# A tuned attention-and-gate kernel: the first x tile in halves, rstd by a GpSimd power, and h chunks begun on two token tiles

**Chip, cores, metric.** One core of one Trainium2 chip. The time is the device time of one execution in microseconds (us), as the median of several executions; "span" is the part of it that the profiler covers, from the first to the last instruction. In the kernel before, the time is the span plus some 1.7 us in every execution.

## The reference

x is 2048 tokens by 448 columns in bf16. The result is x + s·g, where both branches read the same LayerNorm of x:

```python
xn = layernorm(x)                       # eps 1e-5
q, k, v = split_heads(xn @ wqkv)        # 16 heads of 28
phi = lambda t: where(t > 0, t + 1, exp(t)) + 1e-6
kv, z = sum_s phi(k) v, sum_s phi(k)    # linear attention, not causal
s = (phi(q) @ kv / (phi(q)·z + 1e-6)) @ wo
h = relu(xn @ w1 + b1) ** 2             # 448 -> 1792
g = silu(h @ w2 + b2)                   # 1792 -> 448
out = x + s * g
```

## The kernel before

A small list scheduler written in Python takes operations with their reads, writes and estimated durations and fixes the order on each engine, and which of the eight PSUM banks each accumulation gets. The main block is groups of four accumulations, shared among K and Q projections (`K0` = keys of token tile 0) and h chunks (`H4` = columns 512 to 639 of h for 512 tokens). The contraction over 448 columns is three steps of 128 rows and one of 64; two accumulations run their 64-row steps in pairs, on the two halves of the array.

The part that the change touches is the head: what must happen before that block can begin. (Cuts are marked `...`; the comments behind `#` are mine.)

```python
add("dve", lambda e, _: e.memset(junk[:, :], 0.0), [], ["junk"], 0.2).prio = -1000
...
def ln_rstd(lo, hi):                       # rstd = exp(-0.5 * ln(var + eps)), both on ScalarE
    add("act", ... activation(out=vep[:, c], in_=mv[:, c, 1], func=AF.Ln, bias=eps5[:, 0:1]) ...)
    add("act", ... activation(out=rstd[:, c], in_=vep[:, c], func=AF.Exp, scale=-0.5) ...)
...
def pe_transpose(si, eng, prio):           # one token tile of xn -> xT, by TensorE
    for c in range(3):
        e.transpose(v[:, c * P : (c + 1) * P], xn[:, si, c * P : (c + 1) * P], ident[:, :])
    e.transpose(v[0:64, 3 * P : 4 * P], xn[:, si, 384:448], ident[:, :])       # the last 64 columns twice,
    return e.transpose(v[64:P, 3 * P : 4 * P], xn[:, si, 384:448], ident[:, :])  # once for each array half
    ...                                    # then the copy PSUM -> xT, on ScalarE or VectorE (eng)
...
order = ["st0", "mv0", "st1", "mv1", "xn0", "st2", "xn1", "mv2", "st3", "mv3", "xT1", "xn2", "xn3", "xT2", "xT3"]
...
warm(10, wide=True)                        # ten 512-column matmuls on junk, for the clock
pe_transpose(0, "act", -100)
warm(2)                                    # two 128-column ones
pe_transpose(1, "dve", at_head["xT1"])

def third_and_fourth():
    pe_transpose(2, "act", -100)
    pe_transpose(3, "dve", at_head["xT3"])

pe_two(kk(0), kk(1), third_and_fourth)     # K0, K1; tiles 2 and 3 stand before their last steps
...
streams = (("H0 H1 H2 H3 K2 H4 K3 H6", ...   # the first groups of four of the block
```

Three names recur below. T0 to T3 are the transposes of the token tiles. K0 and K1 are the first real matmuls. "K2" is the first matmul of the second group, which comes after chunks 0 to 3; from there on both kernels run the same work in the same order. "The hole" is the gap ahead of chunks 4 and 6, which need PSUM banks that chunks 0 to 3 give back.

## Time and profile before

| quantity | value | from |
|---|---|---|
| time, median of the rounds with the changed kernel | 147.98 us (147.73 to 148.15, 4 runs) | timing |
| span of the profiled run | 146.15 us | page |
| first statistics / K0 / K1 / K2 start | 3.72 / 6.92 / 7.59 / 12.69 us | timeline |
| hole before chunks 4 and 6 | 0.12 us | timeline, worked out below |
| K2 to the last TensorE instruction (its modelled end less the prediction's 0.163 us of pipeline) | 129.94 us | trace |

The chain and the strips stand in the prediction. What it doesn't show is how the h block passes to the second group. The timeline: start, duration, engine, line, operation, how many, and in brackets the idle time before it and what ended it.

```profile
12.24 2.42 ACT L660 ACTIVATE r<-pb,b1f 128x512 bf16<-128x512 f32 x4 [0.81 <-PE pb L651]
...
12.69 0.92 PE L601 MATMUL pb<-w_qkv,xT 64*128 64x448 bf16 x8
...
13.56 1.04 PE L651 MATMUL pb<-xT,w 64*128 64x512 bf16 x8
```

Matmul durations overlap, so spacing must be read from starts: four pairs of 448 columns at 0.189 us follow K2 and take 0.756 us, thus chunk 4 could start at 13.45 and does at 13.56. That 0.12 is the hole: ScalarE, which began to empty the first chunks' banks at 12.24, needs some 0.6 us for each.

### The profile page before, as it was taken

What the parts mean: (1) busy time and instruction counts of PE and PEld (TensorE: products, weight loads), DVE (VectorE), ACT (ScalarE), POOL (GpSimd) and SP (SyncE); (2) the same over time, 40 slices, a digit from 0 to 9 for tenths busy, and PEclk for the clock granted to TensorE, in tenths of its full rate; (3) what the DMA queues carried; (4) which work ended last, traced back from release to release, by engine and by line L of the source; (5) the groups of instructions that cost most, each with busy time, mean ns of one, the idle gap of its engine ahead of it and who ended that gap; (6) DMA issues with size and microseconds to landing.
All of it is one profiled execution on the core that took longest, in us unless ns stands there. A gap on an engine that the chain in (4) does not pass through costs nothing.

```text
span 146.1 us, 3240 instructions
## 1 busy us (share of the span) xinstructions
PE 141.3 (97%) x1330; PEld 69.2 (47%) x1330; DVE 97.2 (67%) x224; ACT 79.8 (55%) x154; POOL 21.2 (14%) x39
## 2 busy tenths in 40 slices
PE   6999999999999999999999999999999999999990
PEld 2344446644444446443545535545555555555440
DVE  0979688888978995999995594973052341604583
ACT  3557799889887888889797191613030220301310
POOL 6000000000000000008900000000050505144140
PEclk9999999999999999999999999999999999999999
DMA  4997649995301100000000000000001011020122
GB/s 124 307 332 215 161 88 350 307 204 112 72 4 36 36 4 0 0 0 4 0 0 0 4 0 0 7 0 0 0 17 51 31 36 63 0 65 2 63 94 94
DMA packets 15513, 10.54 MB, mean 72 GB/s; under 512 B 7244, under 2 KB 15116, under 8 KB 15500
## 3 DMA queue, kind: packets, MB, share of 16 engines
q1 hardware_dynamic: 15040, 9.89, 26.5%
q10 hardware_dynamic: 460, 0.46, 0.9%
q8 instruction: 10, 0.16, 0.5%
q14 instruction: 3, 0.02, 0.1%
HBM read 6.94 MB, written 1.84 MB: 60 GB/s over the span
## 4 chain that ended last, share of the span: by engine, by line
PE 93%; DVE 3%; DMA 2%; issue 0%; DVEq 0%
PE pb L651 29%; PE pb L852 29%; PE pb L601 7%; PE pb L912 7%; PE pb L683 6%; PE pb L623 6%; DMA x_tok<-in_A_x_dram 2%; PE pb L638 1%; DVE st L447 1%; PE pb L689 1%; PE pb L830 1%; PE pb L775 1%; PE pb L741 1%; PE pb L803 1%; PE pb L930 1%; PE pb L490 1%
## 5 line engine op out<-in xcount | busy, mean ns | idle before, releaser
L651 PE MATMUL pb<-xT,w 64*128 64x512 bf16 x392 | 51.6, 376 | 0.1
L852 PE MATMUL pb<-w,r 64*128 64x448 bf16 x448 | 48.2, 349 | 0.0
L660 ACT ACTIVATE r<-pb,b1f 128x512 bf16<-128x512 f32 x56 | 35.0, 689 | 9.0 <-PE pb L651 8.9
L852 PEld LDWEIGHTS pb<-w,r 64*128 64x128 bf16 x448 | 22.8, 94 | 21.0 <-PE pb L852 0.6
L651 PEld LDWEIGHTS pb<-xT,w 64*128 64x128 bf16 x392 | 21.7, 94 | 21.7 <-ACT r L660 0.7
L870 ACT ACTIVATE gbuf<-gbuf 128x448 bf16<-128x448 bf16 x15 | 8.3, 577 | 35.7 <-DVE gbuf L860 35.7
L860 DVE TENSOR_TENSOR gbuf<-pb,b2b 128x448 bf16<-128x448 f32 x15 | 8.7, 621 | 25.4 <-PE pb L852 25.4
L899 POOL TENSOR_TENSOR obuf<-obuf,x_tok 128x448 bf16<-128x448 bf16 x12 | 12.1, 1029 | 57.4 <-DVE obuf L889 57.4
L601 PE MATMUL pb<-w_qkv,xT 64*128 64x448 bf16 (+1 forms) x106 | 16.0, 350 | 0.0
L623 PE MATMUL pb<-xT,w_qkv 64*128 64x512 bf16 x84 | 15.6, 376 | 0.0
L668 DVE TENSOR_TENSOR r<-r 128x512 bf16<-128x512 bf16 x37 | 13.7, 443 | 0.0
L912 PE MATMUL pb<-msb,pqT 64*128 64x448 bf16 x90 | 13.6, 349 | 0.0
L669 ACT ACTIVATE r<-r 128x512 bf16<-128x512 bf16 x19 | 11.3, 633 | 0.0
L447 DVE BATCH_NORM_STATS2 st<-x_tok 128x6 f32<-128x448 bf16 x16 | 9.4, 611 | 2.5 <-DMA x_tok<-in_A_x_dram 2.5
L889 DVE TENSOR_TENSOR obuf<-pb,gbuf 128x448 bf16<-128x448 f32 (+1 forms) x17 | 9.6, 593 | 2.2 <-PE pb L852 1.7
L579 ACT ACTIVATE pk<-pb 128x448 bf16<-128x448 f32 x16 | 8.1, 540 | 3.6 <-PE pb L601 2.9
L591 DVE SCALAR_TENSOR_TENSOR pk<-pb,pk 128x448 bf16<-128x448 f32 x16 | 9.8, 622 | 0.4
L378 POOL MEMSET ehd<- 128x896 bf16 x1 | 0.8, 844 | 62.9 <-DVE zb L613 62.9
L839 DVE TENSOR_TENSOR pqT<-pqT,pb 128x512 bf16<-128x512 bf16 x12 | 7.7, 684 | 3.1 <-PE pb L830 3.1
L683 PE MATMUL pb<-pk,xn 128*128 128x448 bf16 x48 | 9.6, 353 | 0.0
L601 PEld LDWEIGHTS pb<-w_qkv,xT 64*128 64x128 bf16 (+1 forms) x106 | 6.8, 94 | 5.1 <-DVE xT L500 0.4
L623 PEld LDWEIGHTS pb<-xT,w_qkv 64*128 64x128 bf16 x84 | 6.3, 94 | 4.3
(90 smaller groups left out, 117.5 us busy)
## 6 DMA issues: line engine op xcount, KB each, us to landing
out_dram<-obuf SPq DMA_DIRECT2D x15, 112.0 KB, 1.7
w<-in_B_w_dram SPq DMA_DIRECT2D x1, 1568.0 KB, 9.5
x_tok<-in_A_x_dram SPq DMA_DIRECT2D x3, 448.0 KB, 4.4
w_qkv<-in_A_wqkv_dram SPq DMA_DIRECT2D x3, 336.0 KB, 4.8
w<-in_B_w_dram SPq DMA_DIRECT2D x2, 384.0 KB, 4.6
w<-in_B_w_dram SPq DMA_DIRECT2D x1, 576.0 KB, 5.7
w_o<-in_A_wo_dram SPq DMA_DIRECT2D x1, 392.0 KB, 10.8
w_qkv<-in_A_wqkv_dram SPq DMA_DIRECT2D x6, 56.0 KB, 4.3
```

The costliest lines, as they stand in the source:

```text
L447: "dve", lambda e, _: e.bn_stats(st6[:, si, :], x_tok[:, si, :]), [("x", si)], [("st", si)], 0.553
L591: lambda e, _: e.scalar_tensor_tensor(out=slot, in0=ps(buf)[0:rows, 0:n], scalar=1.0 + 1e-6, in1=slot, op0=ALU.add, op1=ALU.max),
L601: return e.matmul(ps(b)[:, 0:D], xT[half[h], c, si * P : (si + 1) * P], w_qkv[half[h], c, D : 2 * D], start=start, stop=stop,)
L623: return e.matmul(ps(b)[:, 0:512], w_qkv[half[h], c, m * P : (m + 1) * P], xT[half[h], c, g * 512 : (g + 1) * 512], start=start, stop=stop,)
L651: return e.matmul(ps(b)[:, 0:512], w_1[half[h], c, fi * P : (fi + 1) * P], xT[half[h], c, g * 512 : (g + 1) * 512], start=start, stop=stop,)
L660: lambda e, _: e.activation(out=slot, in_=ps(b)[:, 0:512], func=AF.Relu, bias=b1f[:, fi : fi + 1]),
L668: return e.tensor_tensor(out=slot, in0=slot, in1=slot, op=ALU.mult)
L669: return e.activation(out=slot, in_=slot, func=AF.Square)
L683: last = e.matmul(ps(b)[:, 0:D], xn[:, si, c * P : (c + 1) * P], pk[:, si, :], start=(si == 0), stop=(si == NT - 1),)
L852: return e.matmul(ps(b)[:, 0:D], r2[half[h], fi, si * P : (si + 1) * P], w_2[half[h], fi, :], start=start, stop=stop)
L899: eng, lambda e, _: e.tensor_tensor(out=ob, in0=ob, in1=x_tok[:, si, :], op=ALU.add),
L912: return e.matmul(ps(b)[:, 0:D], q, msb[half[h], k, :], start=start, stop=stop)
```

## The change

The intent is to shorten the head. Its parts: (1) the warm-up matmuls read a constant that exists from the start, so VectorE needn't fill `junk`, and there are 9 wide and 4 narrow ones in place of 10 and 2; (2) the first x tile is loaded as two halves of 64 partitions on two queues; (3) rstd comes from two GpSimd operations, an add and a power, for every tile; (4) all four transposes of a tile are on 128 columns, GpSimd copying the twin of the last 64, and every copy to xT is on ScalarE; (5) four h chunks begin on the 256 tokens of tiles 0 and 1, between the transposes of tiles 2 and 3, and take the other 256 tokens afterwards. The order of VectorE's head is forced. The diff's core:

```diff
-        load_x(0, 1, "act")
+        for eng, r in (("sp", half[0]), ("act", half[1])):
+            dma(eng, x_tok[r, 0, :], x_r[r, 0, :], [("x", 0, r.start)], 64 * D * 2)
...
-                "act", ... activation(out=vep[:, c], in_=mv[:, c, 1], func=AF.Ln, bias=eps5[:, 0:1]), ...
-                "act", ... activation(out=rstd[:, c], in_=vep[:, c], func=AF.Exp, scale=-0.5), ...
+                "pool", ... tensor_scalar_add(vep[:, c], mv[:, c, 1], 1e-5), ...
+                "pool", ... tensor_tensor(out=rstd[:, c], in0=vep[:, c], in1=power[:, 0 : hi - lo], op=ALU.pow), ...
...
+            part((0, 1, 2), [("xn", si)])
+            part((3,), [("xd", si), b])          # xd: the twin columns, copied by GpSimd
...
-        warm(10, wide=True)
-        pe_transpose(0, "act", -100)
-        warm(2)
-        pe_transpose(1, "dve", at_head["xT1"])
...
-        pe_two(kk(0), kk(1), third_and_fourth)
+        warm(9, wide=True)
+        pe_transpose(0, -100)
+        warm(4)
+        pe_transpose(1, -100)
+        first = [hh(0, fi, 0) for fi in range(4)]                   # tokens 0 to 255
+        second = [hh(0, fi, 1, first[fi].bank) for fi in range(4)]  # tokens 256 to 511, same banks
+        mains(k0)
+        mains(k1)
...
+        mains(first[0])
+        pe_transpose(2, -100)
+        mains(first[1])
+        mains(first[2])
+        pe_transpose(3, -100)
+        mains(first[3])
+        rests(k0, k1, True, True)
...
+        pe_four(*second)
...
-            ("H0 H1 H2 H3 K2 H4 K3 H6", "H5 ...
+            ("K2 H4 K3 H6", "H5 ...
```

## The prediction

> **What bounds the kernel now.** I read the page's busy shares first, then the strip of forty slices, then the chain of waits over the first 14 us, then the timeline of the head. From the page:
>
> ```profile
> PE 141.3 (97%) x1330; PEld 69.2 (47%) x1330; DVE 97.2 (67%) x224; ACT 79.8 (55%) x154; POOL 21.2 (14%) x39
> ...
> PE   6999999999999999999999999999999999999990
> ...
> DVE  0979688888978995999995594973052341604583
> ACT  3557799889887888889797191613030220301310
> ...
> PE 93%; DVE 3%; DMA 2%; issue 0%; DVEq 0%
> ```
>
> The reader should see that TensorE never rests after the first slice, and that 93% of the chain that ended last is TensorE. Start-to-start spacing proves this better than busy time: from 9.65 us on, a 512-column pair of half-array matmuls follows the next every 0.216 us and a 448-column pair every 0.189 us. I laid every matmul end less a fixed 0.163 us of pipeline against the next start; from 9.65 us to the last one at 142.6 us the holes add up to 2.4 us, and most of those are 0.09 us changes of array layout. So the kernel is a head, a solid TensorE block of 133 us, and a tail of some 3.5 us. Only the head has slack to win. A head shortened by x moves the whole block by x, if the block's own inputs come earlier too.
>
> The chain in the head, in order of time:
>
> ```profile
> 0.81 2.89 DMA x_tok<-in_A_x_dram
> ...
> 3.72 0.64 DVE st L447
> ...
> 4.38 0.18 DVE mv L450
> 4.57 0.52 DVE st L447
> ...
> 5.11 0.18 DVE mv L450
> 5.29 0.28 DVE xn L469
> 5.58 0.54 DVE st L447
> 6.11 0.31 DVE xn L469
> ...
> 6.98 1.35 PE pb L601 x6
> 8.33 0.17 PE pb L490 x3
> ...
> 9.17 0.43 DVE xT L500
> ...
> 9.65 3.20 PE pb L651 x28
> ```
>
> The first x tile takes 2.89 us to land; statistics and normalisation of two tiles follow; K0 and K1 (the six L601 matmuls) start at 6.9 us; then TensorE transposes tiles 2 and 3 and, at 9.17, waits for their copy, because the first h chunks (L651) need all four tiles. The rstd link, and the first copy, stand in the timeline:
>
> ```profile
> 4.60 0.29 ACT L458 ACTIVATE vep<-mv,eps 128x1 f32<-128x1 f32 x1 [0.83 <-DVE mv L450]
> ...
> 4.93 0.20 ACT L462 ACTIVATE rstd<-vep 128x1 f32<-128x1 f32 x1
> ...
> 5.90 0.24 PE L491 MATMUL pb<-ident,xn 128*64 128x128 bf16 x1
> ...
> 6.19 0.60 ACT L501 ACTIVATE xT<-pb 128x512 bf16<-128x512 bf16 x1 [0.33 <-PE pb L492]
> ...
> 7.15 0.39 DVE L500 COPY xT<-pb 128x512 bf16<-128x512 bf16 x1
> ```
>
> **What the Trainium skill says.** (1) "TensorE: Matmul & The Clock Gate", Part 1: a cold array passes N columns in N/1.2 ns, a warm one in N/2.4 plus 2.5 ns, and it warms after a window of about 3.4 us that is not tied to the kernel's start. The trace agrees: the warm-up matmuls are 0.427 us apart, later 512-column ones 0.216, and the full clock is recorded from 5.56 us. (2) "SBUF — State Buffer", "Can I just issue two DMAs to hit both halves?": two concurrent DMAs on the two partition halves came out only 6% faster than one. So halves should win little; no run here shows it yet. (3) "Perfetto Trace Analysis", GPSIMD Engine Instruction: reported GpSimd spans are unreliable, start-to-start spacing is the measure. Here four dependent 128x32 selects on GpSimd fill 1.05 us, thus 0.26 each. (4) "SBUF — State Buffer", "Who interferes with whom": a VectorE op in a two-port mode excludes GpSimd from the port pair for its whole length. The normalisation is such a candidate; the statistics are not. The old trace has no GpSimd work beside it, so it cannot say.
>
> **The change part by part.**
>
> Warm-up: the junk memset on VectorE (0.27 us, TensorE released at 1.25) goes, since the ones constant exists before the program starts. TensorE can begin near 0.9; nine matmuls of 0.427 end at 4.8 instead of 5.7. That takes nothing off the path: transposes waited for data at 5.63.
>
> First x tile: 57 KB on each of two queues instead of 112 KB on one. Old landings: 3.70 for tile 0 on ACT's queue, 3.53 for tile 1 on SP's. Since the fixed part dominates, I take 3.4 for the later half, 0.3 earlier; statistics start at 3.4.
>
> rstd: two ScalarE ops take from the end of mv, 4.56, to the start of xn, 5.21: 0.65 us. Two dependent GpSimd ops of 0.26 (the selects' spacing; one element should cost less, a power more) plus hops make about 0.6. I call it even, slightly better. The new VectorE order is st0 mv0 st1 xn0, with mv1 behind xn0, saving 0.10. By the old spacings (st to mv 0.66, mv to st 0.11): mv0 ends 4.24, xn0 starts 4.85 and ends 5.2 (old 5.57).
>
> Transposes on 128 columns: the two 64-column ones cost a layout change of 0.09 us before and 0.12 after. The twin columns they now need come from a GpSimd copy of 128x64; a 128x128 copy there took 0.46, so I estimate 0.3 plus a hop, 0.35. So T0's last transpose runs at 5.6, its eviction 5.85 to 6.45, and K0 begins at 6.55 (old 6.92). K's weights landed at 6.1 before, so they are just not in the way.
>
> Second tile: mv1 follows xn0 (0.29 later) and ends at 5.3; 0.6 on, xn1 at 5.9 (old 6.03). st2 sits before it and needs tiles 2 and 3, old landing 5.29. The twin 0.35, the transposes, and an eviction now on ScalarE at 0.60 instead of VectorE's 0.39, put xT1 at 7.57 (old 7.54), so K1 starts at 7.68 (old 7.59). Here nearly all of the gain made so far is lost again.
>
> Order of TensorE: this is the part that wins. From K1's start the old head needs 7.59 to 12.69 = 5.10 us to reach K2. In the new order the first 256 columns of four h chunks are placed among the transposes of tiles 2 and 3, so that those tiles' LayerNorm and eviction is hidden. Warm work from K1 on: K1 3x0.189 = 0.57; bias transpose 0.06; four chunks of 3x0.109 = 1.31; T2 and T3 8x0.056 = 0.44; one layout change 0.10; K rests 0.19; h rests 2x0.109 = 0.22; second columns 14x0.109 = 1.53. Sum 4.42. Total h work is unchanged: 1.31 + 0.22 + 1.53 = 3.06 against 14x0.216 = 3.02. I add 0.2 for w1 (its last piece landed at 8.03, just where H0 wants it, and SP has one issue more ahead of it) and for xT3. K2 then begins at 7.68 + 4.62 = 12.3 instead of 12.69: 0.4 us won.
>
> Beyond the head: ScalarE drops twenty tiny ops, 4.9 us of its 79.8, and gets two xT evictions, 1.2, and two more squares, 1.3. VectorE loses two copies, the memset and two squares (about 1.9 us). Both are near 85% busy from 9.65 to 66 us under a full TensorE, so this only makes the block safer. One hole of 0.12 us at 13.56, a PSUM bank waiting for an h eviction, may go or move. Tail unchanged. Sum: about -0.4 for the head and -0.1 for such holes.
>
> **The rivals.**
> - K1 replaced by a worse wait: if the power costs 0.6 us or more, or the two-port normalisations shut GpSimd out, each of rstd0 and rstd1 slips by 0.3 to 0.5, the twins too, and K1 starts at 8.3 or later; the head then ends where it did or later: 147.9 to 148.5. For it: no GpSimd power stands in the old trace. Against: only one or two elements per partition, and VectorE is in statistics meanwhile.
> - w1 becomes the bound: in the old trace the DMA engines are saturated from 4.5 us on (near 320 GB/s), so w1's first block cannot come much before 8.0. Should it slip by 0.4 behind the additional issue, H0 starts at 8.4 and I lose 0.2: 147.6. This also caps what a faster rstd could bring, for everything after K1 stands behind H0.
> - The array stays cold longer: the warm-up is 0.4 us shorter, starts earlier and leaves a pause of 0.5 us before the first transpose. If the clock's window ends later than K0's start, the six K matmuls cost up to 1.1 us more: 148.3. The small spread of the old runs (147.73 to 148.08) speaks against a strongly phase-dependent start.
> - Everything goes well: the halves land at 3.2, GpSimd's pair takes 0.4 in place of 0.6. K1 starts at 7.2 and K2 at 11.9: 147.0.
>
> **Range and chances.** 147.88 - 0.5 gives 147.4. The rivals span 147.0 to 148.5, with the favourable side likelier as an easy 0.3 us stands in the second tile; 8 in 10 for 146.8 to 148.0. Two per cent is 2.96 us; TensorE from K2 on to the end, 133 us, is untouched, so to win it the head would have to lose a third of its 9 us, while a loss of 3 us needs a disorder down the block. Hence 0.02, 0.97, 0.01.
>
> **What would show it.** Right if x's first statistics start near 3.4 us; the mv-to-xn link is near 0.6; K0 starts near 6.5 and K1 near 7.7; TensorE shows no hole over 0.3 us from H0 to K2, and K2's first matmul stands 0.3 to 0.6 us earlier than 12.69 while the spacing after it is the same. Wrong if K2 moves by one amount and the span by another (then the block has taken or given time), if the full clock comes after 7 us, or if H0 waits on w1 by more than 0.3 us.

## The result, and the profile after

The changed kernel took 149.81 us in the median (149.18 to 151.11, 4 runs) against 147.98 (147.73 to 148.15, 4 runs) for the kernel before. The ratio is 1.0137 with a 95% interval of 1.009 to 1.0185: slower, by less than 2%, and outside the predicted 146.8 to 148.0.

The profiled spans are 147.89 and 146.15, 1.74 us apart. First the strips of the changed kernel's page, in forty slices of 3.7 us:

```profile
PE   7499999999999999999999999999999999999990
...
POOL 2566202100310000005920000000040505044140
PEclk9959999999999999999999999999999999999998
```

and the clock strip of the kernel before:

```profile
PEclk9999999999999999999999999999999999999999
```

TensorE's second slice is 4 tenths busy where it was 9, GpSimd is busy there where it wasn't, and in the third slice the granted clock, at 9 in all forty slices before, shows 5. Then the chain of waits of the changed kernel (start, length, what):

```profile
0.82 2.44 DMA x_tok<-in_A_x_dram
...
3.36 0.64 DVE st L454
...
4.02 0.20 DVE mv L455
4.21 0.08 issue
4.29 0.24 POOL vep L462
4.54 0.07 issue
4.61 0.59 POOL rstd L467
5.20 0.03 issue
5.23 0.41 DVE xn L474
...
5.69 0.24 POOL xn L485
5.93 0.20 POOL vep L462
...
6.20 0.59 POOL rstd L467
...
6.82 0.41 DVE xn L474
...
7.88 2.31 PE pb L608 x6
...
13.98 1.27 ACT r L671 x2
15.25 0.05 issue
15.30 0.82 PE pb L662 x5
```

Three things stand out. GpSimd's pair (L462, L467) is on the chain twice, once for each of the first two tiles. The six K matmuls take 2.31 us where the same six took 1.35. And the chain now passes through two ScalarE evictions (`ACT r`) into chunk 4. The timeline says what TensorE did meanwhile:

```profile
5.68 0.53 PE L500 MATMUL pb<-ident,xn 128*128 128x128 bf16 x4 [1.36 <-DVE xn L474]
...
7.27 0.61 PE L500 MATMUL pb<-ident,xn 128*128 128x128 bf16 x4 [0.83 <-DVE xn L474]
...
7.79 2.40 PE L608 MATMUL pb<-w_qkv,xT 128*128 128x448 bf16 x6
...
14.10 0.92 PE L608 MATMUL pb<-w_qkv,xT 64*128 64x448 bf16 x8
...
15.30 1.04 PE L662 MATMUL pb<-xT,w 64*128 64x512 bf16 x8 [0.28 <-ACT r L671]
```

It waited 1.36 us for the first tile and 0.83 for the second. K2 starts at 14.10, 1.41 later than before. The hole is 15.30 − (14.10 + 0.756) = 0.44, before 0.12. From K2 to the end TensorE needs 130.27 us, before 129.94. So the whole difference of 1.74 is 1.41 at K2 and 0.33 in the hole, and nothing else in the 130 us after it.

The clock is read in stretches. In the trace, it rose to full at 3.65, fell to half at 7.06 and rose again at 10.47: steps of 3.41 us. The busy times by stretch, for those two (length, then the busy time of PE, PEld, DVE, ACT and POOL with their counts, the granted clock, DMA share and GB/s):

```profile
3.65:7.06 3.41, 1.43 (x11) 0.55 (x9) 2.26 (x7) 1.23 (x2) 1.83 (x5) 1.00 1.08 317
7.06:10.47 3.41, 3.20 (x13) 1.59 (x14) 1.75 (x7) 0.74 (x2) 2.03 (x7) 0.50 0.98 312
```

A step in which TensorE was busy for 1.43 of 3.41 us was followed by one at half clock. In the kernel before, the step from 5.56 has 3.31 of 3.41.

### The profile page after: what moved, and what is told of

Its sections match the earlier page's. It is cut to its first block, busy times and chain, and to the rows that moved or that the text cites. A ratio compares the mean times of both kernels' runs of the same rounds, so it can differ in the third digit from the quotient of the medians.

```text
span 147.9 us, 3266 instructions
## 1 busy us (share of the span) xinstructions
PE 141.1 (95%) x1343; PEld 70.6 (48%) x1343; DVE 94.8 (64%) x219; ACT 77.9 (53%) x138; POOL 31.3 (21%) x64
## 4 chain that ended last, share of the span: by engine, by line
PE 92%; DMA 2%; DVE 2%; POOL 1%; ACT 1%; issue 0%; DVEq 0%
PE pb L662 29%; PE pb L865 29%; PE pb L608 7%; PE pb L925 7%; PE pb L696 6%; PE pb L630 6%; DMA x_tok<-in_A_x_dram 2%; PE pb L645 1%; PE pb L702 1%; PE pb L843 1%; ACT r L671 1%; PE pb L788 1%; POOL rstd L467 1%; PE pb L500 1%; PE pb L754 1%; PE pb L816 1%
## 5 line engine op out<-in xcount | busy, mean ns | idle before, releaser
L662 PE MATMUL pb<-xT,w 64*128 64x512 bf16 (+2 forms) x408 | 52.3, 365 | 0.3 <-ACT r L671 0.3
L662 PEld LDWEIGHTS pb<-xT,w 64*128 64x128 bf16 (+1 forms) x408 | 23.1, 94 | 21.1 <-ACT r L671 1.0
L608 PE MATMUL pb<-w_qkv,xT 64*128 64x448 bf16 (+1 forms) x106 | 17.0, 362 | 0.0
L679 DVE TENSOR_TENSOR r<-r 128x512 bf16<-128x512 bf16 x35 | 13.1, 444 | 1.3 <-ACT r L671 1.3
L680 ACT ACTIVATE r<-r 128x512 bf16<-128x512 bf16 x21 | 12.6, 636 | 0.0
L474 DVE TENSOR_SCALAR xn<-x_tok,mv,rstd 128x448 bf16<-128x448 bf16 x16 | 5.8, 394 | 5.7 <-POOL rstd L467 5.6
```

The source lines that it names most:

```text
L608: return e.matmul(ps(b)[:, 0:D], xT[half[h], c, si * P : (si + 1) * P], w_qkv[half[h], c, D : 2 * D], start=start, stop=stop,)
L662: return e.matmul(ps(b)[:, c0 : c0 + n], w_1[half[h], c, fi * P : (fi + 1) * P], xT[half[h], c, t : t + n], start=start, stop=stop,)
L679: return e.tensor_tensor(out=slot, in0=slot, in1=slot, op=ALU.mult)
L680: return e.activation(out=slot, in_=slot, func=AF.Square)
```

## The experiments

The theory after reading the two traces: two costs, each making the other larger. GpSimd's power makes the mv-to-xn link long (1.03 us, from 4.20 to 5.23, where it was 0.65), twice in series; and the shorter, earlier warm-up leaves TensorE idle in front of it, so that the clock falls back. The rivals: that one of the two does all of it, that the halved load delays the loads behind it, and that the new order of TensorE is itself bad. "The kernel before" in each set is its median in the same rounds.

### First set: the pauses, and ScalarE's rstd

**a_warm**: the changed kernel with TensorE's pauses filled.

```diff
-        warm(9, wide=True)
+        warm(12, wide=True)
         pe_transpose(0, -100)
-        warm(4)
+        warm(14)
```

> The changed kernel with the pauses of TensorE before K0 filled: 12 wide warm-up matmuls instead of 9, and 14 narrow ones instead of 4 between the first two transposes; nothing else. Theory 'clock' (TensorE fell back to the half clock at 7.06 us because it idled in the window before, so that K0, K1 and the bias transpose took 2.5 us instead of 1.2): the clock stays full from its first rise, and the time falls by 1.0 to 1.3 us, from 149.8 to about 148.6; the spread between runs shrinks. Rival 'chain' (the slow GpSimd rstd alone sets the start of K0 and the clock is only a symptom that costs nothing): no change, 149.6 to 150.0, or worse by the overshoot of the fillers.

Measured: 148.93 (148.78 to 149.16, 6 runs) against 147.86, ratio 1.0068 (1.0054 to 1.0083). The same stretch as above is now:

```profile
3.65:7.06 3.41, 3.41 (x23) 1.83 (x22) 2.27 (x7) 1.18 (x2) 1.82 (x5) 1.00 1.01 310
```

In this run the clock rose only at 6.26, so that stretch is not one of its own clock steps; the step after its rise is

```profile
6.26:9.67 3.41, 3.29 (x33) 2.08 (x32) 1.59 (x6) 1.38 (x3) 2.17 (x7) 1.00 0.93 285
```

The clock stayed full from 6.26 on, and K2 moved from 14.10 to 13.30. Over the kernel before, 1.83 became 1.07, so the pauses cost 0.76; the spread of the runs went from 1.9 to 0.4. More than half of the loss remains, so the clock isn't the whole of it.

**a_act**: the changed kernel with rstd on ScalarE again, for all tiles, warm-up as changed.

```diff
-                "pool", ... tensor_scalar_add(vep[:, c], mv[:, c, 1], 1e-5) ...
-                "pool", ... tensor_tensor(out=rstd[:, c], in0=vep[:, c], in1=power[:, 0 : hi - lo], op=ALU.pow) ...
+                "act", ... activation(out=vep[:, c], in_=mv[:, c, 1], func=AF.Ln, bias=eps5[:, 0:1]) ...
+                "act", ... activation(out=rstd[:, c], in_=vep[:, c], func=AF.Exp, scale=-0.5) ...
```

> The changed kernel with rstd back on ScalarE (logarithm and exponential) for all tiles; the warm-up stays at 9 and 4. Theory 'chain': the link from the end of mv to the start of xn falls from 1.03 us to 0.65, twice on the path, K0 starts 0.8 us earlier (7.0), and the time falls by 0.8 to about 149.0. Theory 'clock' adds: with shorter pauses the clock may hold, in some or all runs, then 147.4 to 147.9; if it falls back, 149. So a spread over 1 us between runs would itself speak for the clock.

Measured: 150.37 (149.81 to 151.41, 6 runs), ratio 1.0173 (1.0146 to 1.02): a miss, it got worse. The clock fell back here too, over 8.16 to 11.57, after this stretch:

```profile
4.75:8.16 3.41, 1.93 (x16) 0.94 (x15) 2.56 (x9) 2.20 (x7) 0.47 (x2) 1.00 0.95 276
```

So ScalarE's rstd alone doesn't save the clock. Here the second tile's link was not free to shorten: in VectorE's forced order the statistics of tiles 2 and 3 stand ahead of xn1 and waited for their load:

```profile
6.10 0.63 DVE L454 BATCH_NORM_STATS2 st<-x_tok 128x6 f32<-128x448 bf16 x1 [0.67 <-DMA x_tok<-in_A_x_dram]
```

Thus xn1 began at 6.64 (6.02 in a_act_warm, next) and K0 at 7.59, not 7.0. Of the 0.56 us that a_act is worse than the changed kernel, 0.3 is in the spans (medians 148.4 and 148.1), the rest outside them. The next run shows what else went wrong.

**a_act_warm**: both edits (11 wide, 8 narrow).

> Both mended: rstd on ScalarE and the pauses filled (11 wide and 8 narrow matmuls). If the two causes are separate and add up: K0 near 7.0, full clock, K2 near 12.2, time 147.3 to 147.6, below the kernel before by about 0.4, with a small spread. If the clock is nothing, the same as the run with rstd on ScalarE alone.

Measured: 150.17 (149.49 to 152.28, 6 runs, one of them slow and left out of the ratio), ratio 1.0151 (1.0112 to 1.0189): a miss again, although K0 began at 7.01 and K2 at 12.36, before the kernel before's 12.69. Its timeline:

```profile
10.92 1.15 DVE L454 BATCH_NORM_STATS2 st<-x_tok 128x6 f32<-128x448 bf16 x2 [2.33 <-DMA x_tok<-in_A_x_dram]
...
12.32 0.30 ACT L463 ACTIVATE vep<-mv,eps 128x2 f32<-128x2 f32 x1 [1.55 <-DVE mv L455]
...
14.93 1.04 PE L662 MATMUL pb<-xT,w 64*128 64x512 bf16 x8 [1.65 <-ACT r L671]
```

x's tiles 4 to 7 landed at 10.89, in the kernel before at 9.17. Their Ln stands in ScalarE's order ahead of the exponentials of K and the evictions of h; ScalarE waited 1.55 us in front of it with those evictions behind it, and chunk 4 came late. (Of the five fast executions, with spans of 146.9 to 148.1, two have 3.4 and 3.7 us outside their span, so 150.17 overstates what the head does.) The gain of a faster rstd was thus turned into a new wait, because loads came later. This is the rival of the late loads, though not on the path where I had looked for it.

**b_warm9**: the kernel before with the new warm-up alone.

```diff
-        add("dve", lambda e, _: e.memset(junk[:, :], 0.0), [], ["junk"], 0.2).prio = -1000
+        junk = nc.const_aps.tensor(1.0, [P, 512], bf)
...
-        warm(10, wide=True)
+        warm(9, wide=True)
         pe_transpose(0, "act", -100)
-        warm(2)
+        warm(4)
```

> The kernel before with the new warm-up alone: constant ones for junk, start at 0.84 us, 9 wide matmuls instead of 10, 4 narrow instead of 2. Theory 'clock': its pause of about 1 us before the first transpose makes the clock fall back in some of the runs, so a spread over 0.7 us and a median 0.2 to 1.2 us above the kernel before. Rival: if the warm-up is harmless (the pauses made by the slow GpSimd link are needed as well), 147.9 within 0.2.

Measured: median 147.82, ratio 1.0033 (0.9988 to 1.0078); but four executions lie at 147.73 to 147.89 and two at 149.42 and 149.55, a split that no set of the kernel before shows. In the traced run, one of the four, the step after the clock's rise at 4.26 was

```profile
4.26:7.67 3.41, 2.40 (x20) 1.06 (x19) 3.31 (x12) 2.33 (x9) 0.00 (x0) 1.00 1.05 310
```

and the clock held. Taken together: 1.43 and 1.93 us busy of 3.41 were followed by half clock, 2.40 and 3.29 were not. But busy time alone doesn't decide it, for a later step of a_act_warm held less than the 1.93 of a_act, and the clock stayed full after it:

```profile
12.13:15.55 3.42, 1.77 (x22) 0.80 (x19) 3.30 (x13) 3.17 (x9) 0.00 (x0) 1.00 0.68 215
```

One reading fits every trace: without the transposes, the three steps that half clock followed hold 1.06 us (changed kernel), 0.61 (after5) and 1.06 (a_act) of matmul, and no other full-clock step in the 17 traces holds less than the 1.50 of b_warm9's above. No run tested that reading.

The two slow executions were not traced. Their mean granted clock is 0.996, where one step at half clock would make it 0.988 (worked out under after5), so they are not such a lapse. A first rise that comes late would leave no mark in that mean, which doesn't count the time before it: a_order's clock rose only at 6.86, and its mean is 1.000. Which it was here stays open.

### Second set: the halves, and the order of transposes

**a_hact_warm**: ScalarE's Ln and Exp for the four head tiles only, GpSimd's pair for tiles 4 on, so that nothing on ScalarE waits for the late tiles; pauses filled (11 wide, 10 narrow).

```diff
         def ln_rstd(lo, hi, prio=None):
+            if hi - lo == 1:
+                add("act", ... AF.Ln ...)
+                add("act", ... AF.Exp, scale=-0.5 ...)
+                return
```

> The changed kernel with rstd on ScalarE for the four head tiles only (the later tiles keep GpSimd, so ScalarE's queue no longer holds a logarithm that waits for x tiles 4 to 7 ahead of the evictions, as it did in the run with rstd on ScalarE for all tiles) and with the pauses filled (11 wide, 10 narrow). Theory 'chain and clock add up': against the run with filled pauses alone (148.93) the two links of 1.03 us become 0.65, K0 starts near 7.0 instead of 7.9, and the 1.8 us hole of the earlier run is gone: 147.6 to 148.1, a spread under 0.5 us. Rival 'the loads': if the hole is made by the late landing of x tiles 4 to 7 itself, 148.5 or more remains.

Measured: 148.64 (148.07 to 149.33, 6 runs) against 148.08, ratio 1.0042 (1.0018 to 1.0066). K2 stands at 12.67 and the hole is 0.45; x's tiles 4 to 7 still landed only at 11.02. The w1 weights had become a bound too: they landed at 8.79, and chunk H0, at 8.84, waited 0.19 us for them. That is the prediction's second rival.

**a_whole_warm**: a_warm with the first tile loaded whole, on the ACT queue.

```diff
-        for eng, r in (("sp", half[0]), ("act", half[1])):
-            dma(eng, x_tok[r, 0, :], x_r[r, 0, :], [("x", 0, r.start)], 64 * D * 2)
+        load_x(0, 1, "act")
```

> The changed kernel with filled pauses (12 and 14, as in the run with 148.93) and the first x tile whole on ScalarE's queue again. Theory 'halves cost': with two halves SP has one more issue ahead of all weights (w1's last piece 8.5 instead of 8.0, x tiles 4 to 7 after 9.6 to 11.8 instead of 9.2), which costs more than the 0.3 us gained on the first landing where GpSimd's link hides part of it: 148.6 to 148.9 and tiles 4 to 7 near 9.3. Rival 'halves pay': K0 starts 0.3 later and the time is 149.2.

Measured: 148.94 (148.81 to 149.02, 5 runs), ratio 1.006 (1.0048 to 1.0072). With the power in place the halves are worth nothing: K2 is at 13.31, as in a_warm. (In these two traces the first tile landed alike, with the first statistics at 3.49 and 3.50.)

**a_hact_whole_warm**: ScalarE's rstd for the head tiles, whole first tile, pauses filled: of the change, the new order, the 128-column transposes and the ScalarE copies are left in the head, and GpSimd's pair for tiles 4 on (11 wide, 10 narrow).

> ScalarE's rstd for the head, the whole first tile and filled pauses together: what is left of the change is the order of TensorE with h on two tiles, the 128-column transposes with GpSimd twins, and GpSimd's rstd for later tiles. K0 near 7.2, K2 near 12.4 against 12.69 of the kernel before: 147.5 to 147.8, a little below the kernel before. If the halves pay, this is 0.3 above the same run with halves.

Measured: 147.91 (147.72 to 148.10, 5 runs), ratio 0.9992 (0.9979 to 1.0005): level with the kernel before. Against a_whole_warm, which differs in rstd and the warm-up lengths fitted to it, that is 1.03 us; K2 came from 13.31 to 12.38. Against a_hact_warm, which differs in the halves, it is 0.73, of which 0.65 is in the spans (medians 146.1 and 146.75). 0.29 of that stands at K2, where a_hact_warm had waited for w1; the rest was not followed to a wait. Its timeline:

```profile
12.38 0.92 PE L619 MATMUL pb<-w_qkv,xT 64*128 64x448 bf16 x8
...
13.58 1.04 PE L673 MATMUL pb<-xT,w 64*128 64x512 bf16 x8 [0.28 <-ACT r L682]
```

K2 is 0.31 earlier than before, and the hole, 13.58 − 12.38 − 0.756 = 0.44, is 0.32 longer. The new order and the wide transposes together gain what was promised, and the order's own hole takes it back.

**a_order**: the same with the old transposes, two of them on 64 columns.

```diff
-            part((0, 1, 2), [("xn", si)])
-            part((3,), [("xd", si), b])
+                for c in range(3):
+                    e.transpose(v()[:, c * P : (c + 1) * P], xn[:, si, c * P : (c + 1) * P], ident[:, :])
+                e.transpose(v()[0:64, 3 * P : 4 * P], xn[:, si, 384:448], ident[:, :])
+                return e.transpose(v()[64:P, 3 * P : 4 * P], xn[:, si, 384:448], ident[:, :])
```

> As the run before it, but with the old transposes (two of 64 columns, no twin copies on GpSimd). Tells the transposes' part: if the wide ones win 0.1 us each at layout changes, this is 0.1 to 0.3 slower; if the twin copy costs 0.25 us on the path as much as the layout change saves, the same within 0.1.

Measured: 149.05 (148.68 to 149.59, 6 runs), ratio 1.0067 (1.005 to 1.0084). The 1.14 us between the two medians is not a clean measure: 0.6 is in the spans (146.7 and 146.1), the rest outside them, and in the traced run the clock rose only at 6.86, and the ten narrow warm-up matmuls then ran cold until 7.03 and kept T1 waiting. The part from K0 to K2, free of that, took 5.65 us against 5.16. Of these 0.49, 0.44 stand at the transposes of tiles 2 and 3, which took 0.44 us each in place of 0.22: the price of two changes of array layout at each.

### Third set: repairing the hole, the pause, the power, the transposes

**a_best**: a_hact_whole_warm with chunks 4 and 6 in the banks of K0 and K1, and VectorE normalising tiles 4 to 7 only after it has emptied those two.

```diff
+                    if lo == 4:
+                        norm.after = [freed]          # freed: the last operation of K1's phi
...
+        reuse = {(0, 4): k0.bank, (0, 6): k1.bank}
```

> The best so far (ScalarE's rstd in the head, whole first tile, filled pauses: 147.91, K2 0.3 earlier than in the kernel before but a hole of 0.44 us after it, where h chunks 4 and 6 wait for ScalarE to empty the banks of chunks 0 and 2) with that hole attacked: chunks 4 and 6 take the banks of K0 and K1, and VectorE empties those before it normalises tiles 4 to 7. Theory 'the hole is a bank wait': it falls below 0.1 us and the time to 147.4 to 147.6. Rival: the later normalisation of tiles 4 to 7 (by about 1.5 us) turns into a new wait near 21 to 24 us, and nothing is won.

Measured: 148.34 (147.77 to 149.08, 6 runs) against 147.80, ratio 1.0036 (1.0013 to 1.0059): a miss. K2 came at 12.16, but:

```profile
10.19 1.15 DVE L455 BATCH_NORM_STATS2 st<-x_tok 128x6 f32<-128x448 bf16 x2 [1.58 <-DMA x_tok<-in_A_x_dram]
...
13.08 1.14 DVE L609 SCALAR_TENSOR_TENSOR pk<-pb,pk 128x448 bf16<-128x448 f32 x2
...
14.28 1.04 PE L673 MATMUL pb<-xT,w 64*128 64x512 bf16 x8 [1.20 <-DVE pk L609]
```

VectorE waited for tiles 4 to 7 with their statistics ahead of K's last operation in its order, so the banks of K0 and K1 came free later, at 14.22, than those of chunks 0 and 2 would have: ScalarE had emptied them by 13.31. A bank was exchanged for a worse one in this execution, whose span is 146.9. Three of the six have spans of 146.0 and 146.1, level with the kernel before, so the wait needn't stand in all; they were not traced.

**b_warm12**: the kernel before with an early warm-up without the pause: as b_warm9, but 12 wide.

> The kernel before with the new early warm-up, but 12 wide matmuls in place of 9, so that the pause before the first transpose shrinks from about 1.1 us to nothing when cold. With 9 two of six executions were 1.75 us longer. Theory 'clock lapse by the pause': no execution over 148.4, all near 147.7 to 148.0. Rival (an early start alone makes the second state): again some at 149.5.

Measured: 147.87 (147.65 to 148.41, 6 runs), ratio 1.0005 (0.9988 to 1.0021). No execution near 149.5, so the constant and the early start alone don't make the slow ones, and filling the pause removed them. By which way stays open, since the clock mean of b_warm9's two speaks against a lapse, and six against six executions, two of them slow, is thin.

**a_nopow**: a_warm with a multiply in place of the power. The result is wrong (relative error 0.68); every operation, wait and transfer stays.

```diff
-                ... tensor_tensor(out=rstd[:, c], in0=vep[:, c], in1=power[:, 0 : hi - lo], op=ALU.pow),
+                ... tensor_tensor(out=rstd[:, c], in0=vep[:, c], in1=power[:, 0 : hi - lo], op=ALU.mult),
```

> The changed kernel with filled pauses (148.93) and a multiplication in place of the power on GpSimd; the result is wrong on purpose. The power took 0.58 us for one element per partition, the addition ahead of it 0.23. Theory 'the power itself costs': the second operation falls to about 0.25, the link from mv to xn from 1.03 to 0.70, K0 starts 0.65 earlier, time 148.2 to 148.4. Rival 'two hops over GpSimd cost': the link stays over 0.95 and the time at 148.9.

Measured: 148.33 (148.20 to 148.44, 5 runs) against 147.80, ratio 1.0033 (1.002 to 1.0046), a_warm 1.0068.

```profile
4.32 0.23 POOL L462 TENSOR_SCALAR vep<-mv 128x1 f32<-128x1 f32 x1 [2.57 <-DVE mv L455]
4.63 0.19 POOL L467 TENSOR_TENSOR rstd<-vep,power 128x1 f32<-128x1 f32 x1
4.86 0.40 DVE L474 TENSOR_SCALAR xn<-x_tok,mv,rstd 128x448 bf16<-128x448 bf16 x1
...
7.41 1.30 PE L608 MATMUL pb<-w_qkv,xT 128*128 128x448 bf16 x6 [0.38 <-DMA w_qkv<-in_A_wqkv_dram]
```

The second GpSimd operation takes 0.19 in place of 0.58. K0 came from 7.92 to 7.41, and there waits for its weights: with the power gone, the next bounds are loads, which the halves delay: of the K weights here, and of w1 at H0, which waited 0.17 us at 8.93. So the power alone is worth at least 0.54 of the 1.07 that a_warm loses (0.53 is left).

**b_wideT**: the kernel before with the 128-column transposes and GpSimd twins alone.

> The kernel before with nothing changed but the transposes of the head: four of 128 columns, the twin columns copied by GpSimd. Each tile loses two changes of array layout (0.09 and 0.12 us) and gains a GpSimd copy of 0.24 plus hops on its path. In the undoing run the old transposes cost 1.1 us of the median, 0.8 of it in front of K2. If that holds without the new order, H0 starts 0.2 to 0.4 earlier and the time is 147.5 to 147.7; if the twin copy eats it (tiles 0 and 1 are waited for, tile 3 too), 147.9 to 148.1.

Measured: 147.85 (147.46 to 147.96, 6 runs), ratio 0.9998 (0.9983 to 1.0014). In the traced run K2 was 0.39 earlier, at 12.30, and the span 0.39 shorter, at 145.76; but that run is one of two at 147.46 and 147.48, and the other four are where the kernel before is. Why was not traced. Of the 0.39, 0.1 is a first tile that landed earlier and 0.27 stands at the transposes of tiles 2 and 3 (0.62 us in place of 0.89). On its own, this part is at best a small gain.

### Fourth set: the hole again, and the changed kernel once more

**a_hole**: a_hact_whole_warm with the last quarter of the h chunks' second half moved behind the first steps of K2 and K3, to give ScalarE time.

```diff
-        pe_four(*second)
+        phase((s0, K4), (s2, K4))
+        phase((s1, K4), (s3, K4))
+        phase((s2, K3), (s0, K3))
+        phase((k2, K4), (k3, K4))
+        phase((s3, K3), (s1, K3))
+        phase((h4, K4), (h6, K4))
+        ...
```

> The run at 147.91 (ScalarE's rstd in the head, whole first tile, filled pauses) with one thing moved on TensorE: the last quarter of the four h chunks comes after the first quarter of K2 and K3, so that chunks 0 and 2 are complete 0.33 us earlier in relation to chunks 4 and 6, which take their banks. Theory 'hole is a bank wait on ScalarE's evictions, made by the half-width second columns': the hole of 0.44 us falls to 0.1 to 0.15 as in the kernel before, from K2's block to the end of TensorE's work 0.3 us less, time 147.5 to 147.7. Rival (ScalarE is late for another reason): the hole stays 0.4.

Measured: 147.87 (147.77 to 149.20, 7 runs) against 147.96, ratio 1.000 (0.9984 to 1.0015). The traced execution is the one of 149.20, but its span is 146.1 like the others'; the excess lies outside it. The hole stayed at 0.44:

```profile
12.00 0.92 PE L619 MATMUL pb<-w_qkv,xT 64*128 64x448 bf16 x8
...
12.75 0.49 PE L673 MATMUL pb<-xT,w 64*128 64x256 bf16 x6
...
13.52 1.04 PE L673 MATMUL pb<-xT,w 64*128 64x512 bf16 x8 [0.28 <-ACT r L682]
```

The expectation was a slip of mine: the move changed the order of the work between the end of chunks 0 and 2 and the start of chunk 4, not its amount. That work is 0.327 us of h pairs (half as wide as before) and 0.756 of K pairs, 1.08 in all, plus the hole of 0.44: 1.52. In the kernel before the h pairs are full width, 0.65 + 0.756 + 0.12: 1.52 too. In these traces chunk 4 starts 1.5 us after the last matmul of chunks 0 and 2, for two ScalarE evictions (1.27 us in the chain above), and by halving the second columns the change shortened what covers it by 0.32, the growth of the hole.

**a_top**: a_hole with the copy of tile 1 to xT on VectorE, and ahead of other work there.

> The same, with tile 1's transposed copy on VectorE (0.39 us) instead of ScalarE (0.60), as in the kernel before: K1 0.15 to 0.2 earlier. 147.3 to 147.6; faster than the kernel before in every fast execution if both hold. If VectorE's copy pushes xn2 and xn3 back so that T2 waits, nothing is won over the run beside it.

Measured: 147.71, five executions from 147.60 to 147.84 and one of 148.81, against 147.96 (147.75 to 148.22); ratio 0.9995 (0.9972 to 1.0017). The excess of the one execution lies outside its span, which is 145.9 like the others'; the spans' median is 145.9 against 146.2. That is the best version found, 0.25 in the median, and the interval doesn't exclude zero.

**after5**: the changed kernel again, unedited, five rounds.

> The changed kernel again, for its distribution over more executions and another trace. Theory 'clock lapse': most executions 149.2 to 151.2, none near 148.9 unless the clock's windows fall so that no lapse comes; the trace shows one window of 3.41 us at half clock between 5 and 12 us, or a first rise after 7 us. Rival: a stable time near 149.8 with the clock full from before K0 in its trace.

Measured: 149.53 (149.48 to 150.21, 5 runs) against 147.96, ratio 1.0123 (1.0104 to 1.0142). The executions form two groups: 150.15 and 150.21 with a mean granted clock of 0.987, and 149.48 to 149.53 with 0.996. The traced one is of the first, and its clock is half from 7.97 to 11.39. One step of 3.41 us at half clock is a mean of 1 − 1.71/148.4 = 0.988, so the 0.987 is that lapse. What the second group lost, with no such lapse in its mean, was not traced and stays open (a first rise that comes late would not show in the mean, as under b_warm9); that filling the pauses made every execution 148.78 to 149.16 in a_warm says only that it hangs on the pauses too. The same holds for the longest execution of the first measurement, 151.11 with a mean clock of 1.000: a lapse doesn't explain it.

## Why the prediction was wrong

The bound was read rightly: a head and a solid TensorE block. So was the place to look, K2 against 12.69 and the spacing after it. The sum failed in four terms. It put K1 at 7.68 and K2 4.62 later, at 12.3; K1 came at 8.86, 1.18 late, and K2 5.24 after it, 0.62 more, at 14.10.

**The rstd link, "about 0.6. I call it even, slightly better".** This is the largest. I sized the power by the selects' 0.26; it takes 0.58, the add 0.23, and the three hand-overs 0.22, together 1.03. It stands twice in series, and the second time the twin copy delays the add as well, so xn1, put at 5.9, began at 6.82. The price of the GpSimd pair in the head is 1.03 us (a_hact_whole_warm against a_whole_warm), of which the power itself is about 0.54 (a_nopow). The prediction's first rival had it: "if the power costs 0.6 us or more", with K1 at 8.3 or later. In a_warm, where the clock holds, K1 is at 8.63.

**The warm-up, "takes nothing off the path", "a pause of 0.5 us".** Nothing was gained, but a lot was lost: with the long link the pause became 1.36 and a second of 0.83 followed. The step held 1.43 us of work, and the clock fell back while K0 and K1 ran: six matmuls 0.373 apart in place of 0.189 cost 1.1 us, and K2 is 0.80 later than in a_warm, where the clock held. This was the third rival, put at 148.3 by itself. I weighed the rivals as alternatives, but the slow power widens the pause that the clock then fails in, so they came together. Their losses, 0.5 to 1.1 and 0.9 over my 147.4, add to 148.8 to 149.4, outside the range.

**K0 "begins at 6.55".** T1 stands ahead of K0 in TensorE's order, so K0 can't begin before xn1, its twin and T1. I had worked out T1's time, later than 6.55, in the next paragraph and didn't hold the two together. K1 is the one that counted, so this slip hid the series of two links and cost nothing by itself.

**"One hole of 0.12 us [...] may go or move", "-0.1 for such holes".** It grew to 0.44. I counted ScalarE's load over the block, and not what covers the two evictions that chunk 4 waits for; the halved second columns cover 0.32 less.

What held: the first statistics at 3.4 (3.36, in part by luck: the seven traces with halves have 3.36 to 3.54 and the ten with the whole tile 3.49 to 3.74, some 0.17 apart in the mean and not 0.3); "halves should win little" (nothing, and in a faster chain they cost 0.73 with the loads behind them coming later); K1 to K2 in 4.62 us at full clock (a_warm: 13.30 − 8.63 = 4.67, before 5.10), though not by the reordering alone; the block after K2 untouched but for the hole. From K1 to K2 the traces have 4.81 with the wide transposes alone (b_wideT), 4.89 with the new order and the old transposes (a_order), and 4.45 with both (a_hact_whole_warm). The second rival, w1 as the next bound, came true only where the head was faster: H0 waited for it in a_hact_warm (0.19) and a_nopow (0.17).

I had also feared that VectorE's normalisation would shut GpSimd out. Nothing shows it: the power takes 0.58 both beside the statistics at 4.61 and with VectorE idle at 6.20. But in no trace did a power of the head run beside a normalisation, so it stays untested. Two slips of the prediction cost nothing: its block of 133 us counts from 9.65, not from K2 (129.94), and a half is 56 KB, not 57.

In medians over the kernel before, the loss of 1.83 us is: pauses 0.76 (changed kernel to a_warm), halves about 0.2 across two sets and not distinguishable from zero by their ratios (1.0068 and 1.006), rstd 1.03 (to a_hact_whole_warm), less 0.17 that the rest is ahead, which is not distinguishable from zero either (0.9992). With after5 for the changed kernel the loss is 1.57 and the pauses' share 0.50. The split also depends on the order in which one takes the parts away: with the fast rstd the halves cost 0.73 (0.65 in spans).

## What to carry to other kernels

Size an operation that the old trace doesn't hold by a run of its own before trusting a sum to it, and count how often it stands in series in front of the first consumer in each engine's order. Treat a shorter warm-up and a slower producer as one question, for what the producer adds to the pause is what the clock may fail on; warm-up work that ends just before the data comes is nearly free. When work is moved ahead of a wait, ask what used to cover the next wait: the 0.31 us that the new order and the wide transposes won at K2 came back as a hole longer by 0.32.

## What the Trainium skill lacked or had wrong

- "GPSIMD Engine Reference", 3.1 (Elementwise), gives cycles per element and names a dispatch, but no figure for a power. Here one element per partition took 0.58 us, two took about 0.72, where the add took 0.23 and a multiply 0.19 in its place; each hand-over between engines added 0.04 to 0.09.
- "TensorE: Matmul & The Clock Gate", Part 1, has the array cold after an idle window of some 3.4 us, which the steps of 3.41 us here agree with in length. But the window needn't be idle: 1.43, 1.49 (after5) and 1.93 us of modelled busy time in 3.41 were followed by half clock, with no pause over 1.4 us in the changed kernel. Nor does busy time alone decide it, for 1.77 us in a step of a_act_warm was not. The Part tells of a clock that falls back on short idles, but gives no figure for how much work a window must hold.
- "SBUF — State Buffer", "Can I just issue two DMAs to hit both halves?", speaks of bandwidth. For latency, the later half of 56 KB landed 2.4 to 2.6 us after issue over the traces, where the whole tile of 112 KB took 2.6 to 2.9; yet the issue of x's tiles 4 to 7, behind one issue more on the same queue, moved from 4.77 to 5.50 us. That section has nothing on this price.
- "TensorEngine Tiling (Array Packing)", Key Properties, says that a change of tiling mode drains TensorE and gives no time. In the kernel before, the change to 64-column transposes and back cost 0.09 and 0.12 us, and without it the transposes of tiles 2 and 3 took 0.22 us each in place of 0.44 (a_hact_whole_warm against a_order).
- No page says how long the bank of a finished accumulation is out of use: here 1.5 us from the last matmul of two chunks to the first into their banks, for two ScalarE evictions of 128x512.
